# Row thresholds on VectorE, and four chunks transposed on TensorE: one change to a fused attention and feed-forward kernel

## The chip, the cores and the metric

One core of a Trainium2 chip. The metric is the device time of one execution in microseconds (us). Engines are named as in the profile: PE is TensorE, PEld its weight loads, DVE VectorE, ACT ScalarE, POOL GpSimd, SP SyncE, which here issues DMAs. All runs told of here were at a granted TensorE clock of 0.994 or more (0.998 or more in the profiled ones). Calls can land on different chips: the kernel before took 568.0, 570.0 and 567.5 us in three groups of runs, so kernels are compared by their ratio to the kernel before in the same rounds.

## The reference

```python
scores = q @ k.T / sqrt(64)                      # 8 batches x 8 heads, 576 x 576
thresh = max(scores, axis=-1) - tau              # tau = 0.02
scores = where(scores >= thresh, scores, -1e9)
x = softmax(scores) @ v                          # heads side by side: 4608 x 512
xn = x / sqrt(mean(x * x) + 1e-6) * rms_g
out = (silu(xn @ w_gate) * (xn @ w_val)) @ w_out # 512 -> 1536 -> 512
```

## The kernel before

The work is cut into 144 **steps** (128 query rows of two heads) and 36 **chunks** (128 rows of all eight heads, four steps). A step multiplies the scores into PSUM (`s_ps`, one buffer per head), VectorE copies them to SBUF as -score/8 and keeps each row's minimum in `mx`, and a tiny operation adds tau to it:

```python
nc.vector.tensor_tensor_reduce(                       # L589, once per head
    out=ssb[a][:, h], in0=s_ps[h][...], in1=zrow, scale=-1.0 / 8.0, scalar=3.0e38,
    op0=ALU.add, op1=ALU.min, accum_out=mx[m][:, h:h + 1])

def nthr(o):                                          # L596, the row threshold, 128x2
    nc.gpsimd.tensor_scalar(out=nth[m], in0=mx[m], scalar1=tau, scalar2=None, op0=ALU.add)
```

ScalarE then takes exponentials with `nth` as bias. From step 16 on, every second step leaves one head's mask to GpSimd: a comparison with `nth` ("mask", L640, 1.73 us) and a product with the exponentials ("take", L645, 1.28 us). After attention GpSimd norms a chunk's rows, and a transposing DMA (DMA_TRANSPOSE in the trace: in the median 1.2 us of the issuing queue and 2.5 us to landing) brings them to the feed-forward part (FFN):

```python
nc.sync.dma_start_transpose(out=xnT[slot][:, :, off:off + 128], in_=xn[ci % 2])   # L738, if ci >= N_XPE
...  # if ci < N_XPE: four TensorE transposes into PSUM, one VectorE copy to xnT
```

The order of instructions on each engine is not written by hand. The kernel lists all operations with a cost in nanoseconds (a table `COST`), plays them through a small list scheduler when it is built, and emits each engine's instructions in the order that comes out. So a changed entry in this table moves no work, but can move the order everywhere.

## Time and profile before

| | kernel before |
|---|---|
| time, median | 568.0 us (567.1 to 568.9, 5 runs) |
| TensorE, VectorE, ScalarE, GpSimd busy | 98%, 75%, 80%, 57% |
| threshold | 144 x 220 ns on GpSimd |
| transposes of normed rows | 36 by DMA |
| first FFN matmul | at 49.9 us |

A busy share is the time in which an engine shows an instruction, over the span. The threshold in the groups of instructions (busy us, mean ns, idle time before and what ended it):

```profile
L596 POOL TENSOR_SCALAR nth<-mx 128x2 f32<-128x2 f32 x144 | 31.6, 220 | 133.9 <-DVE mx L589 120.6
```

### The profile page before, as it was taken

What the parts mean: (1) busy time and instruction counts of PE and PEld (TensorE: products, weight loads), DVE (VectorE), ACT (ScalarE), POOL (GpSimd) and SP (SyncE); (2) the same over time, 40 slices, a digit from 0 to 9 for tenths busy, and PEclk for the clock granted to TensorE, in tenths of its full rate; (3) what the DMA queues carried; (4) which work ended last, traced back from release to release, by engine and by line L of the source; (5) the groups of instructions that cost most, each with busy time, mean ns of one, the idle gap of its engine ahead of it and who ended that gap; (6) DMA issues with size and microseconds to landing.
All of it is one profiled execution on the core that took longest, in us unless ns stands there. A gap on an engine that the chain in (4) does not pass through costs nothing.

```text
span 568.3 us, 13686 instructions
## 1 busy us (share of the span) xinstructions
PE 558.4 (98%) x5000; PEld 334.7 (59%) x5000; DVE 427.2 (75%) x1093; ACT 457.4 (80%) x739; POOL 322.4 (57%) x462
## 2 busy tenths in 40 slices
PE   8999999999999999999999999999999999999997
PEld 4666766767676555555555555545555455454674
DVE  4899977969958588758895789659875886586354
ACT  4999899999878787979898898778978897884332
POOL 2378946976747457666766658555666555551000
PEclk9999999999999999999999999999999999999999
DMA  8999998769994686999876799789887565633211
GB/s 187 250 289 282 178 195 184 161 132 202 167 202 104 136 159 149 177 177 187 178 160 148 142 186 181 161 168 162 174 167 184 88 96 86 178 81 44 84 37 38
DMA packets 270019, 88.98 MB, mean 157 GB/s; under 512 B 252544, under 2 KB 262272, under 8 KB 269952
## 3 DMA queue, kind: packets, MB, share of 16 engines
q1 hardware_dynamic: 267168, 86.02, 74.1%
q0 software_dynamic: 1600, 1.57, 1.8%
q8 instruction: 39, 0.64, 0.5%
q10 hardware_dynamic: 1184, 0.52, 0.3%
q14 instruction: 28, 0.23, 0.1%
HBM read 37.75 MB, written 9.44 MB: 83 GB/s over the span
## 4 chain that ended last, share of the span: by engine, by line
PE 89%; DVE 3%; DMA 2%; issue 2%; ACT 2%; POOL 1%; SPq 0%; DVEq 0%; POOLq 0%; ACTq 0%
PE s_ps L566 28%; PE ring L792 16%; PE ring L797 16%; PE ring L853 14%; PE ring L697 6%; PE ring L303 2%; PE ring L693 2%; DVE ssb L589 2%; DMA qkn<-in_q_dram 1%; PE s_ps L831 1%; PE s_ps L853 1%; PE ring L659 1%; PE s_ps L797 1%; PE ring L364 1%; DMA stage<-in_q_dram 1%
## 5 line engine op out<-in xcount | busy, mean ns | idle before, releaser
L589 DVE CUSTOM_DVE_ANT_0 ssb<-s_ps,zrow 128x576 f32<-128x576 f32 x288 | 207.8, 754 | 67.7 <-PE s_ps L566 60.5
L607 ACT ACTIVATE ssb<-ssb,nth 128x576 f32<-128x576 f32 x224 | 165.9, 766 | 32.4 <-POOL nth L596 32.1
L566 PE MATMUL s_ps<-qkt 64*128 64x288 f32 x1024 | 170.2, 429 | 1.4 <-DVE mx L589 1.1
L566 PEld LDWEIGHTS s_ps<-qkt 64*128 64x128 f32 x1024 | 96.2, 186 | 53.5 <-DVE mx L589 16.2
L640 POOL TENSOR_SCALAR wsb<-ssb,nth 128x576 f16<-128x576 f32 x64 | 110.5, 1726 | 9.7 <-DMA wt<-wsb 2.9
L792 PE MATMUL ring<-xnT,wg 128*128 128x512 f16 (+1 forms) x548 | 112.9, 328 | 0.4 <-DVE sl L809 0.4
L797 PE MATMUL ring<-xnT,wv 128*128 128x256 f16 (+1 forms) x544 | 111.4, 327 | 0.6 <-ACT qTv L472 0.3
L596 POOL TENSOR_SCALAR nth<-mx 128x2 f32<-128x2 f32 x144 | 31.6, 220 | 133.9 <-DVE mx L589 120.6
L809 DVE SCALAR_TENSOR_TENSOR sl<-th,ring 128x512 f32<-128x512 f32 (+1 forms) x137 | 75.9, 554 | 25.9 <-ACT th L806 24.6
L614 ACT ACTIVATE wsb<-ssb 128x1152 f16<-128x1152 f32 x80 | 92.9, 1161 | 1.9
L806 ACT ACTIVATE th<-ring 128x512 f32<-128x512 f32 (+1 forms) x137 | 66.3, 486 | 28.9 <-PE ring L792 26.4
L853 PE MATMUL ring<-wo,hf 128*128 128x512 f16 x384 | 89.3, 380 | 0.0
L645 POOL TENSOR_TENSOR wsb<-wsb,esb 128x576 f16<-128x576 f16 x64 | 81.8, 1278 | 8.8 <-ACT esb L626 4.4
L814 DVE TENSOR_TENSOR hf<-ring,sl 128x256 f16<-128x256 f32 (+1 forms) x136 | 75.9, 558 | 10.0 <-PE s_ps L566 0.5
L797 PEld LDWEIGHTS <-wv 128*128 128x128 f16 x576 | 52.2, 98 | 42.9 <-issue 12.3
L792 PEld LDWEIGHTS <-wg 128*128 128x128 f16 x576 | 52.0, 98 | 41.0 <-issue 11.6
L853 PEld LDWEIGHTS <-hf 128*128 128x128 f16 x408 | 37.4, 98 | 47.2 <-issue 6.6
L626 ACT ACTIVATE esb<-ssb,nth 128x576 f16<-128x576 f32 x64 | 49.2, 768 | 7.1 <-POOL nth L596 7.0
L697 PE MATMUL ring<-va,wt 128*128 128x65 f16 (+1 forms) x1264 | 52.8, 193 | 0.0
L697 PEld LDWEIGHTS <-wt 128*128 128x128 f16 (+1 forms) x1280 | 48.7, 100 | 3.4
L611 ACT ACTIVATE wsb<-ssb 128x576 f16<-128x576 f32 x64 | 43.6, 681 | 1.6
L693 PE MATMUL ring<-va,wt 128*128 128x130 f16 (+1 forms) x158 | 35.1, 227 | 0.1
(68 smaller groups left out, 448.1 us busy)
## 6 DMA issues: line engine op xcount, KB each, us to landing
vst<-in_v_dram SPq DMA_DIRECT2D x32, 256.0 KB, 3.2
qkn<-in_k_dram SPq DMA_DIRECT2D x31, 256.0 KB, 3.8
out_dram<-osb SPq DMA_DIRECT2D x31, 256.0 KB, 2.6
qkn<-in_q_dram SPq DMA_DIRECT2D x28, 256.0 KB, 4.1
stage<-in_moe_w_gate_dram SPq DMA_DIRECT2D x6, 512.0 KB, 6.6
stage<-in_moe_w_val_dram SPq DMA_DIRECT2D x6, 512.0 KB, 6.3
wt<-wsb SPq DMA_TRANSPOSE x128, 3.1
wo<-in_moe_w_out_dram POOLq DMA_DIRECT2D x4, 384.0 KB, 7.6
```

Of the source, the lines that this page charges most:

```text
L566: nc.tensor.matmul(s_ps[h][rows, ROW_AT + n * part:ROW_AT + n * part + n], lhs(hs), kT[i][p][h][hs, n * part:n * part + n], start=True, st ...
L589: nc.vector.tensor_tensor_reduce(out=ssb[a][:, h], in0=s_ps[h][:, ROW_AT:ROW_AT + S], in1=zrow, scale=-1.0 / 8.0, scalar=3.0e38, op0=ALU.a ...
L607: nc.scalar.activation(out=ssb[a][:, h], in_=ssb[a][:, h], func=PRELU, scale=-1.0, bias=nth[m][:, h:h + 1], **PRELU_KW)
L614: nc.scalar.activation(out=wsb[s % NW], in_=ssb[a], func=AF.Exp)
L640: nc.gpsimd.tensor_scalar(out=wsb[s % NW][:, h], in0=ssb[a][:, h], scalar1=nth[m][:, h:h + 1], scalar2=None, op0=ALU.is_le)
L645: nc.gpsimd.tensor_tensor(out=wsb[s % NW][:, h], in0=wsb[s % NW][:, h], in1=esb[es], op=ALU.mult)
L697: nc.tensor.matmul(ring[o.slot[0]][rs, at:at + D + 1], w[:, 5 * h + j, rs], va[vi][:, p, 2 * j + h], start=False, stop=(h == 1 and j == 3))
L792: nc.tensor.matmul(ring[o.slot[0]][:, 0:n], wg[d][:, fs], xnT[slot][:, d, 0:n], start=(d == 0), stop=(d == 3))
L797: nc.tensor.matmul(ring[o.slot[0]][:, 0:n], wv[d][:, fs], xnT[slot][:, d, 0:n], start=(d == 0), stop=(d == 3))
L809: nc.vector.scalar_tensor_tensor(out=sl[i][:, 0:n], in0=th[i][:, 0:n], scalar=1.0, in1=ring[g.slot[0]][:, 0:n], op0=ALU.add, op1=ALU.mult)
L814: nc.vector.tensor_tensor(out=hf[hi][:, 0:n], in0=ring[vv.slot[0]][:, 0:n], in1=sl[i][:, 0:n], op=ALU.mult)
L853: nc.tensor.matmul(ring[(first or o).slot[0]], hf[hs[fc][0]][:, 128 * j:128 * (j + 1)], wo[:, fc], start=(fc == 0), stop=(fc == NFC - 1))
```

## The change

It moves the threshold from the busy queue of GpSimd to VectorE, which has just made its input, so that ScalarE gets it sooner; it frees the early DMA queue of four DMA transposes so that the FFN can start earlier; and it brings three issue costs of the ordering table nearer to what was seen.

```diff
-    sp=480.0, sp_v=650.0, ..., sp_qk=900.0, ...
+    sp=420.0, sp_v=600.0, ..., sp_qk=680.0, ...
@@
-            nc.gpsimd.tensor_scalar(out=nth[m], in0=mx[m], scalar1=tau, scalar2=None, op0=ALU.add)
-        tn = add("POOL", COST["pool_tiny"], s - 4, ...)
+            (nc.gpsimd if NTH == "POOL" else nc.vector).tensor_scalar(
+                out=nth[m][:, lo:hi], in0=mx[m][:, lo:hi], scalar1=tau, scalar2=None, op0=ALU.add)
+        tns.append(add("POOL" if NTH == "POOL" else "DVE", ... else NTHC, s - 4, ...))
@@
+NTH = 'DVE'
+NTHC = 80.0
@@
-N_XPE = 0
+N_XPE = 4
```

(With `NTH = 'DVE'` there is one threshold operation per step, for both heads, as before.)

More of the change, by code (lines that the diff above doesn't have):

```diff
@@ L20 @@
     pool_tiny=270.0, pool_mean=800.0, pool_dma=850.0, cast_v=650.0, cast_vt=420.0, cast_w=720.0,
-    sp=480.0, sp_v=650.0, sp_w=600.0, sp_tr=1300.0, sp_qk=900.0, sp_tl=630.0,
+    sp=420.0, sp_v=600.0, sp_w=600.0, sp_tr=1300.0, sp_qk=680.0, sp_tl=630.0,
 )
@@ L593, in emit_softmax, with nthr @@
             ttr_of[s, h] = add("DVE", COST["ttr"], s - 1, [so, o_c] + exp_of.get(s - NSS, []), ttr)
-        def nthr(o):
-            nc.gpsimd.tensor_scalar(out=nth[m], in0=mx[m], scalar1=tau, scalar2=None, op0=ALU.add)
-        tn = add("POOL", COST["pool_tiny"], s - 4, [ttr_of[s, 0], ttr_of[s, 1]], nthr)
+        tns = []
+        for lo, hi in ((0, 1), (1, 2)) if NTH == "EACH" else ((0, 2),):
+            def nthr(o, lo=lo, hi=hi):
+                (nc.gpsimd if NTH == "POOL" else nc.vector).tensor_scalar(
+                    out=nth[m][:, lo:hi], in0=mx[m][:, lo:hi], scalar1=tau, scalar2=None, op0=ALU.add)
+            tns.append(add("POOL" if NTH == "POOL" else "DVE", COST["pool_tiny"] if NTH == "POOL" else NTHC, s - 4,
+                           [ttr_of[s, h] for h in range(lo, hi)], nthr))
         wfree = [w_read.get(s - NW)]
@@ L614, in ex2 @@
                     nc.scalar.activation(out=wsb[s % NW], in_=ssb[a], func=AF.Exp)
-                pls.append(add("ACT", COST["prelu"], s + 0.5, [tn], prelu))
+                pls.append(add("ACT", COST["prelu"], s + 0.5, [tns[h % len(tns)]], prelu))
                 if ways != "pp":
@@ L627, in ex @@
                                          bias=nth[m][:, h:h + 1])
-                e = add("ACT", COST["exp1"], s + 0.4, [tn, pre.get(("es", es))], ex)
+                e = add("ACT", COST["exp1"], s + 0.4, [tns[h % len(tns)], pre.get(("es", es))], ex)
                 if way == "d":
@@ L646, in take @@
                                                 op=ALU.mult)
-                    mk = add("POOL", COST["mask_g"], s + 0.4, [tn] + wfree, mask)
+                    mk = add("POOL", COST["mask_g"], s + 0.4, [tns[h % len(tns)]] + wfree, mask)
                     st = add("POOL", COST["take_g"], s + 0.4, [e, mk], take)
```

## The prediction

> **What bounds the kernel now.** I read the page from the top: busy shares, then the slices.
>
> ```profile
> PE 558.4 (98%) x5000; PEld 334.7 (59%) x5000; DVE 427.2 (75%) x1093; ACT 457.4 (80%) x739; POOL 322.4 (57%) x462
> ...
> PE   8999999999999999999999999999999999999997
> ...
> DVE  4899977969958588758895789659875886586354
> ACT  4999899999878787979898898778978897884332
> ...
> PEclk9999999999999999999999999999999999999999
> ```
>
> TensorE looks full from the second slice on, at full clock. [...] the groups by shape give 380 ns for one 512-column matmul, while in the chain of waits twelve of them in a row take 2.69 us, 224 ns each. So I asked differently: in the list of instructions in order of time I took, for each kind of TensorE block (eight score matmuls; four gate matmuls; and so on), the time from its start to the start of the next block, and its median: 1.17 us for a score block, 0.87 for four 512-column gate matmuls, 0.44 for four of 256 columns. What a block took above its median I call a stall (for the few kinds that come only a few times, above their shortest pace). The stalls sum to only 34.9 of 568 us: 7.9 before 20 us, 11.1 from 20 to 80, 2.9 from 160 to 180, 4.2 after the last matmul, and 8.8 in all the rest, about 0.5 us in each 20. So TensorE does work almost all of the time, and only stalls can be saved. The order in time shows both states of a score block (start, us, what):
>
> ```profile
> 47.53 1.91 PE L566 MATMUL s_ps<-qkt 64*128 64x288 f32 x8 [0.32 <-DVE mx L589]
> ...
> 304.67 1.24 PE L566 MATMUL s_ps<-qkt 64*128 64x288 f32 x8
> ```
>
> At 304.67 it runs through; at 47.53 its second half waits until VectorE has read the other head's old scores out of PSUM (s_ps is single). The busy times by stretch (PE, PEld, DVE, ACT, POOL, in us of 10 or 20) show why that happens early:
>
> ```profile
> 20.00:30.00 10.00, 9.03 (x127) 7.16 (x126) 9.05 (x26) 9.39 (x15) 3.90 (x8) 1.00 1.06 279
> 30.00:40.00 10.00, 8.94 (x116) 6.79 (x115) 8.95 (x25) 9.17 (x13) 7.99 (x17) 1.00 1.14 283
> 40.00:50.00 10.00, 9.57 (x95) 6.31 (x95) 9.16 (x28) 9.25 (x13) 8.67 (x17) 1.00 1.18 272
> 50.00:60.00 10.00, 10.00 (x111) 7.19 (x110) 9.54 (x29) 9.90 (x17) 7.99 (x15) 1.00 1.13 267
> ```
>
> Until about 60 us VectorE and ScalarE are at 90% and over, the DMA engines too (last two columns: DMA share, GB/s), and TensorE has no FFN work before 49.9 us.
>
> **The waits that the change aims at.** In the view of waits, us in total, times, longest:
>
> ```profile
> POOL nth L596 <- DVE mx L589: 120.6, 68, 9.3
> DVE ssb L589 <- PE s_ps L566: 60.5, 66, 2.6
> ACT ssb L607 <- POOL nth L596: 32.1, 39, 2.0
> ...
> ACT esb L626 <- POOL nth L596: 7.0, 13, 1.8
> ```
>
> ScalarE waits 39.1 us for the threshold, part of it because the 220 ns threshold stands in GpSimd's queue behind masks of 1.73 us and weight casts of 0.69 us. But ScalarE is 80% busy, and these waits hardly reach TensorE: the row above them shows VectorE itself waiting 60.5 us for scores. GpSimd's 120.6 us are idle time of an engine that sets nothing.
>
> **Part 1, 144 thresholds from GpSimd to VectorE.** Removed: 144 x 220 ns = 31.6 us of GpSimd, one hop between engines per step, and the queueing there. Added on VectorE: [...] the trace has 83 ns for the 128x1 accumulator read and 179 for the 128x4 reciprocal from PSUM. I take 80 ns: 144 x 0.08 = 11.5 us, and VectorE goes from 75% to 77%. From 80 us on, where TensorE stalls 0.5 us in 20, the shorter hop has nothing to shorten. Before 80 us ScalarE waits for thresholds 3.9 us between 20 and 80; some 20 steps lie there, so VectorE pays 20 x 0.08 = 1.6 us in the stretch where it is nearly full. I put the gain at 2 us and the cost at 1.5.
>
> **Part 2, four chunks transposed on TensorE.** Removed: 4 of 36 crossbar transposes (1.2 us of the issuing queue each, up to 2.5 early; 2.4 to 5.7 us to landing) out of the stretch with the fullest DMA, and the queue's halts in front of them: at 30, 42 and 55 us SyncE stands still for 1.6 to 3 us until the normed rows are there, with weight and q loads behind. Added: 16 matmuls. [...] this trace has nine transposes of the same shape in 0.51 us, 57 ns each at their pace (219 ns is the modelled length of one), and the measurement counts: 16 x 57 ns = 0.9 us, with about 0.09 us at each change of kind (a 512-column gate block takes 0.96 instead of 0.87 then) 1.3 us in all on the path that sets the end. VectorE gets four copies of 128x512 f16 at 416 ns, 1.7 us, where it is nearly full. In return the first FFN block can start before 49.9 us: its second chunk's normed rows are there at 43.8 us, the crossbar brings them about 2.5 us later; through TensorE and a copy they would be there after about 1 us. I expect the start 2 to 4 us earlier and 2 to 3 us of early stalls filled. q loads that land sooner could save part of one more stall (0.9 us at 35.9 us, where TensorE waits for a q load of 7.5 us).
>
> **Part 3, the static order.** Three costs of issuing are lowered in the table from which the kernel computes the order of all engines. No work changes; the order does, everywhere. With TensorE so full that moves little: I allow 2 us either way.
>
> Sum without a further wait: -2 + 1.5 + 1.3 - 2.5 - 0.5 = about -2 us, and at most some 10, since 11.1 us of early stalls are all there is to win apart from start and end.
>
> **Rivals.** (a) **A lock takes the wait's place.** [...] The kernel before shows nothing of it[...]. Estimate: GpSimd without thresholds is busy 291 us; its instructions, each with half its length as the mean rest (64 x 1.73 squared, 64 x 1.28 squared, the casts, norms and powers: 350 us squared in all), give 350 / 2 / 568 = 0.31 us of expected wait per threshold, 144 x 0.31 = 44 us, and VectorE would be occupied 85%. Most of it would fall into VectorE's waits for scores. From 250 to 300 us, though, VectorE is busy 43.1 of 50 us and would come near 94%; there silu and gate products come late, PSUM slots come free late and TensorE stalls. I let a fifth through: +9 us. (b) **VectorE becomes the early bound**: 3.2 us more work before 80 us lengthen that stretch by as much, and the earlier FFN start gives nothing, since its silu and gate products need VectorE too: +3 us. (c) **Hidden anyway**: the FFN is planned 16 steps behind its chunk, so a crossbar of 2.5 us is covered, and thresholds are off the path: 569 us. (d) **The early stalls go** for the most part: 558 us.
>
> **Range and chances.** Without the lock I get 566; with it about 575. A threshold beside GpSimd's masks would have been tried by whoever tuned this, and be kept only if it paid, so I give full effect of the lock a third or less, and (c) and (d) pull the other way: 567 us, 557 to 580. Over 2% means 11.4 us: as a gain it needs more than all early stalls, 5%; as a loss it needs the lock to reach TensorE with a quarter of its waits, 10%; within 2%, 85%.
>
> **What would show it.** In the changed profile: VectorE's threshold near 80 ns, no wait of ScalarE for GpSimd's threshold, GpSimd's busy time down by some 31 us; if (a) holds, a threshold of several hundred ns on average, long ones ending with GpSimd's mask. TensorE's first gate matmul before 48 us; 32 crossbar transposes of normed rows instead of 36; stalls of the score block between 20 and 60 us fewer if I am right, more under (b). From 80 us on TensorE's blocks at the same pace. I am wrong if TensorE stalls far more than 0.5 us in 20 there, or if the new order opens a gap such as the one at 166 to 176 us.

-2 + 1.5 + 1.3 - 2.5 - 0.5 is -2.2, "about -2 us", and so 566 from 568. The 80 ns behind the 1.5 are my estimate, near the 83 ns of the accumulator read in the trace. Rival (a) is a supposition, that a threshold on VectorE stands until the GpSimd instruction beside it ends, and an estimate of its waits from the lengths of GpSimd's instructions in the trace; the fifth of them that I let through is the +9 us that makes 575 of 566. "Lock" is my name for such a wait, "crossbar" for the transposing DMA.

## The result, and the profile after

The changed kernel took **573.4 us** (573.1 to 574.2, 5 runs) against 568.0 us: ratio 1.0096, 95% interval 1.0079 to 1.0113. A ratio here is the mean time of one kernel's fast runs over that of the other's fast runs of the same rounds, so it is not quite the ratio of the medians. Later the same kernel gave 1.0062 (run f1 below). It is a small loss, within 2%, and it is clear of noise.

The page of the changed kernel, its busy line and three of its costliest groups (busy us, mean ns, idle time before and what ended it):

```profile
PE 561.3 (98%) x5016; PEld 336.4 (59%) x5016; DVE 456.2 (80%) x1241; ACT 461.4 (81%) x739; POOL 290.0 (51%) x318
...
L611 ACT ACTIVATE ssb<-ssb,nth 128x576 f32<-128x576 f32 x224 | 165.7, 766 | 22.2 <-DVE nth L598 21.5
...
L630 ACT ACTIVATE esb<-ssb,nth 128x576 f16<-128x576 f32 x64 | 49.4, 772 | 15.5 <-DVE nth L598 14.9
...
L598 DVE TENSOR_SCALAR nth<-mx 128x2 f32<-128x2 f32 x144 | 34.8, 242 | 4.9
```

GpSimd lost 32.4 us of work, as it should. But VectorE gained 29.0, and the threshold takes 242 ns on average there, more than the 220 ns on GpSimd. ScalarE's wait for it hardly shrank: 21.5 + 14.9 = 36.4 us against 39.1.

The mean hides two kinds. The list of instructions in order of time (start, us, engine, line) shows a long threshold and a short one, 3.7 us apart:

```profile
115.21 1.28 POOL L649 TENSOR_TENSOR wsb<-wsb,esb 128x576 f16<-128x576 f16 x1
...
115.90 0.61 DVE L598 TENSOR_SCALAR nth<-mx 128x2 f32<-128x2 f32 x1
116.43 0.41 DVE L813 SCALAR_TENSOR_TENSOR sl<-th,ring 128x256 f32<-128x256 f32 x1
...
118.95 1.91 PE L566 MATMUL s_ps<-qkt 64*128 64x288 f32 x8
...
119.60 0.17 DVE L598 TENSOR_SCALAR nth<-mx 128x2 f32<-128x2 f32 x1
```

GpSimd's take runs from 115.21 to 116.49. The threshold begins at 115.90, while the take runs, and ends at 116.51, some 25 ns after it; the one at 119.60 finds GpSimd idle and needs 0.17 us. Behind the long one all of VectorE's queue is late, and the next score block to start, at 118.95, runs for 1.91 us: its second half waits. Of the 144 thresholds 111 took 157 to 195 ns, most of them 169 or 170; 33 took over 200 ns, up to 1.29 us, and nearly every one of them ended 22 to 28 ns after a GpSimd instruction: 24 after a take, 4 after a norm, 4 after a cast, 1 around a DMA issue. Taken over the median of 170 ns, the waits sum to 10.4 us. GpSimd's own masks and takes are as long as before (1.72 and 1.28 us on average), so it is VectorE that waits.

### The profile page after: what moved, and what is told of

Same layout as the page of the kernel before. It is cut to its first block, busy times and chain, and to the rows that moved or that the text cites. A ratio compares the mean times of both kernels' runs of the same rounds, so it can differ in the third digit from the quotient of the medians.

```text
span 571.1 us, 13669 instructions
## 1 busy us (share of the span) xinstructions
PE 561.3 (98%) x5016; PEld 336.4 (59%) x5016; DVE 456.2 (80%) x1241; ACT 461.4 (81%) x739; POOL 290.0 (51%) x318
## 4 chain that ended last, share of the span: by engine, by line
PE 88%; DVE 5%; DMA 4%; ACT 1%; issue 1%; SPq 0%; DVEq 0%
PE s_ps L566 27%; PE ring L796 16%; PE ring L801 15%; PE ring L857 15%; PE ring L701 6%; DMA qkn<-in_q_dram 4%; PE ring L303 2%; DVE ssb L589 2%; PE ring L697 2%; PE s_ps L801 1%; PE s_ps L835 1%; PE s_ps L857 1%; DMA stage<-in_q_dram 1%; DVE hf L818 1%; DVE nth L598 1%
## 5 line engine op out<-in xcount | busy, mean ns | idle before, releaser
L611 ACT ACTIVATE ssb<-ssb,nth 128x576 f32<-128x576 f32 x224 | 165.7, 766 | 22.2 <-DVE nth L598 21.5
L796 PE MATMUL ring<-xnT,wg 128*128 128x256 f16 (+1 forms) x564 | 114.5, 325 | 0.1
L801 PE MATMUL ring<-xnT,wv 128*128 128x512 f16 (+1 forms) x520 | 108.2, 330 | 0.2
L813 DVE SCALAR_TENSOR_TENSOR sl<-th,ring 128x256 f32<-128x256 f32 (+1 forms) x141 | 76.7, 544 | 19.9 <-ACT th L810 19.3
L810 ACT ACTIVATE th<-ring 128x256 f32<-128x256 f32 (+1 forms) x141 | 67.5, 480 | 28.4 <-PE ring L796 23.4
L818 DVE TENSOR_TENSOR hf<-ring,sl 128x512 f16<-128x512 f32 (+1 forms) x130 | 73.5, 566 | 10.5 <-PE ring L801 0.9
L630 ACT ACTIVATE esb<-ssb,nth 128x576 f16<-128x576 f32 x64 | 49.4, 772 | 15.5 <-DVE nth L598 14.9
L598 DVE TENSOR_SCALAR nth<-mx 128x2 f32<-128x2 f32 x144 | 34.8, 242 | 4.9
```

The lines of the kernel that those rows point to most:

```text
L611: nc.scalar.activation(out=ssb[a][:, h], in_=ssb[a][:, h], func=PRELU, scale=-1.0, bias=nth[m][:, h:h + 1], **PRELU_KW)
L796: nc.tensor.matmul(ring[o.slot[0]][:, 0:n], wg[d][:, fs], xnT[slot][:, d, 0:n], start=(d == 0), stop=(d == 3))
L801: nc.tensor.matmul(ring[o.slot[0]][:, 0:n], wv[d][:, fs], xnT[slot][:, d, 0:n], start=(d == 0), stop=(d == 3))
L813: nc.vector.scalar_tensor_tensor(out=sl[i][:, 0:n], in0=th[i][:, 0:n], scalar=1.0, in1=ring[g.slot[0]][:, 0:n], op0=ALU.add, op1=ALU.mult)
L818: nc.vector.tensor_tensor(out=hf[hi][:, 0:n], in0=ring[vv.slot[0]][:, 0:n], in1=sl[i][:, 0:n], op=ALU.mult)
```

## The experiments

All were correct. The first eight shared the runs of the kernel before (570.0 us), the last four had their own (567.5 us).

| run | thresholds | transposes on TensorE | issue costs | median us | ratio to before (95%) |
|---|---|---|---|---|---|
| e1 | GpSimd | 0 | new | 566.8 | 0.9951 (0.9934 to 0.9967) |
| e2 | VectorE | 0 | new | 571.9 | 1.0045 (1.0024 to 1.0066) |
| e3 | GpSimd | 4 | new | 568.0 | 0.9976 (0.9957 to 0.9994) |
| e4 | VectorE, as reduction | 4 | new | 569.2 | 0.9986 (0.9969 to 1.0004) |
| f1 | VectorE (the change) | 4 | new | 573.2 | 1.0062 (1.0044 to 1.0080) |
| f2 | reduction, twice | 4 | new | 570.7 | 1.0017 (1.0001 to 1.0032) |
| f3 | reduction, then tensor_scalar | 4 | new | 574.0 | 1.0075 (1.0059 to 1.0092) |
| f4 | VectorE | 4 | old | 577.3 | 1.0141 (1.0111 to 1.0172) |
| g1 | VectorE, cost entry 245 | 4 | new | 571.7 | 1.0067 (1.0049 to 1.0085) |
| g2 | GpSimd | 0 | half way | 568.1 | 1.0007 (0.9987 to 1.0027) |
| g3 | GpSimd | 0 | old, other order | 568.3 | 1.0007 (0.9989 to 1.0025) |
| g4 | GpSimd | 0 | new, other order | 566.6 | 0.9975 (0.9957 to 0.9992) |

My theory after the result was LOCK: the threshold stands until a running take, norm or cast of GpSimd ends, as in the trace above, and this reaches TensorE. What in the hardware makes it stand, no run shows. Its rivals were OWN TIME (any added VectorE time counts), TRANSPOSES, and ORDER (the new table entries gave a worse order).

**One part at a time (e1, e2, e3).**

```diff
 e1: NTH = 'POOL', N_XPE = 0     # only the three issue costs are new
 e2: NTH = 'DVE',  N_XPE = 0
 e3: NTH = 'POOL', N_XPE = 4
```

> Only the three issue costs in the ordering table are new; thresholds on GpSimd, no transposes on TensorE. ORDER theory (the new static order alone loses the 5.3 us): 572 to 574 us. LOCK, OWN TIME and TRANSPOSE theories (the work itself costs it): 567 to 569 us, as before.

> The change without the four transposes on TensorE (all 36 chunks through the crossbar). If the thresholds cost the time (LOCK or OWN TIME): 572 to 573.5 us, threshold mean near 240 ns on VectorE. If the TRANSPOSES cost it: 568 to 569 us. ORDER: about as e1.

> The change with the thresholds back on GpSimd, the four transposes on TensorE. If the TRANSPOSES cost the time: 571 to 574 us. If the thresholds cost it: 567 to 569.5 us (1.1 us of added TensorE work, perhaps won back). ORDER: about as e1.

e1 is not slower but 0.5% faster, so ORDER falls for the three issue costs. From e1 to e3 the transposes cost 1.2 us by the medians, from e1 to e2 the thresholds cost 5.1. Added up, -3.2 + 5.1 + 1.2 = +3.1 us, and the change showed +3.2 on this chip. So the loss is the thresholds, and part of it is hidden by a gain from the costs.

**The same threshold as a reduction (e4).** `mx` gets a second column per head that holds tau, and the threshold is a reduction over the pair. Order and everything else stay: in the traces of f1 and e4 the instructions of VectorE, ScalarE and GpSimd come in the same order, but for six memsets of tau at the start, and TensorE's differ in four records.

```diff
-mx = [sb(f"mx{i}", [128, 2]) ...]
+mx = [sb(f"mx{i}", [128, 2, 2]) ...]              # [:, :, 1] is set to tau once
-    nc.vector.tensor_scalar(out=nth[m], in0=mx[m], scalar1=tau, op0=ALU.add)
+    nc.vector.tensor_reduce(out=nth[m], in_=mx[m], axis=X, op=ALU.add)
```

> The whole change in the same static order, but the threshold is a VectorE reduction over pairs (row extreme, tau)[...]. If LOCK holds: no threshold over 200 ns, none ending with a GpSimd instruction, and the time 569 to 571.5 us. If the waits for the lock are absorbed by VectorE's idle time: thresholds short, yet the time within 0.8 us of the change's 573.4. If there is no such lock: the long thresholds stay.

The view of the tile `nth` of e4, and of the thresholds of the changed kernel (duration in ns: minimum, median, maximum; first and last start):

```profile
L600 DVE TENSOR_REDUCE nth<-mx x144: 145/157/159, 10.0 to 508.2; 128x2 f32<-128x4 f32 x144
```

```profile
L598 DVE TENSOR_SCALAR nth<-mx x144: 157/170/1292, 10.0 to 511.6; 128x2 f32<-128x2 f32 x144
```

No reduction took more than 159 ns. The time fell from 573.2 (f1) to 569.2 us: 4.0 of the 5.1 us that the thresholds cost are gone, in the same order of instructions, so ORDER falls here too. The same step as above, in order of time in e4:

```profile
114.23 0.08 DVE L591 DVE_READ_ACCUMULATOR2_ANT mx<- 128x1 f32 x1
114.23 0.75 DVE L591 CUSTOM_DVE_ANT_0 ssb<-s_ps,zrow 128x576 f32<-128x576 f32 x1
...
114.34 1.28 POOL L650 TENSOR_TENSOR wsb<-wsb,esb 128x576 f16<-128x576 f16 x1
114.91 0.08 DVE L591 DVE_READ_ACCUMULATOR2_ANT mx<- 128x1 f32 x1
115.03 0.16 DVE L600 TENSOR_REDUCE nth<-mx 128x2 f32<-128x4 f32 x1
115.10 0.41 DVE L814 SCALAR_TENSOR_TENSOR sl<-th,ring 128x256 f32<-128x256 f32 x1
...
118.16 1.38 PE L568 MATMUL s_ps<-qkt 64*128 64x288 f32 x8
```

The take runs from 114.34 to 115.62 again, right across the threshold, which takes no notice of it. The next gate product starts at 115.10 instead of 0.5 us later, and the score block at 118.16 runs 1.38 us instead of 1.91.

These lines also show what a short threshold costs VectorE's queue, which is not its recorded length. Without one in between, the next instruction starts together with the accumulator read (114.23); with one, it starts 0.11 us after the read's end (115.10 against 114.99), as the threshold needs what is read. Over the whole traces the next instruction starts 192 ns later in the median for a reduction and 195 for a tensor_scalar that does not wait: nearly the same, so in its own time e4 hardly differs from the change, while the waits are gone.

**Own time or waits (f1, f2, f3).** By the recorded lengths e4 also has 12 us less VectorE time than the change, so I took OWN TIME to be still open. f2 and f3 add 144 operations of nearly equal length (147 and 158 ns in the median) to e4, writing to a tile that nobody reads: f2 reductions, of which none waited in e4 (159 ns at most), f3 tensor_scalars, of which 33 of 144 took over 200 ns in the change. f1 is the change itself on this chip.

```diff
     nc.vector.tensor_reduce(out=nth[m], in_=mx[m], axis=X, op=ALU.add)
+f2: nc.vector.tensor_reduce(out=nth2[m], in_=mx[m], axis=X, op=ALU.add)
+f3: nc.vector.tensor_scalar(out=nth2[m], in0=mx[m][:, :, 0], scalar1=tau, op0=ALU.add)
```

> The changed kernel itself, on the same chip as the three below: 1.010 of before. Everything below is compared with it and with e4's reduction form.

> e4 with every reduction issued twice (the second into an unused tile): 144 x 157 ns = 22.6 us more work on VectorE[...]. OWN TIME theory (VectorE's added microseconds count wherever they come from; e4 to the change is 12 us of VectorE time and 1.1% of time): at least 1.2% over e4. LOCK theory (only the long, bunched waits count): within 0.5% of e4.

> e4 with a tensor_scalar into an unused tile behind every reduction: the threshold itself is early and lock-free[...]. LOCK through VectorE's queue: 0.6 to 1.2% over f2, which has the same count of instructions. LOCK through the late threshold (ScalarE and GpSimd get it late): within 0.3% of f2.

The busy lines of e4, f2 and f3, then the groups by shape of f2 and of f3:

```profile
PE 558.0 (98%) x5016; PEld 334.3 (59%) x5016; DVE 446.2 (79%) x1247; ACT 461.4 (81%) x739; POOL 290.7 (51%) x318
PE 560.7 (99%) x5016; PEld 336.6 (59%) x5016; DVE 453.7 (80%) x1391; ACT 461.0 (81%) x739; POOL 289.9 (51%) x318
PE 562.3 (98%) x5016; PEld 337.2 (59%) x5016; DVE 463.1 (81%) x1391; ACT 461.5 (81%) x739; POOL 290.1 (51%) x318
```

```profile
L601 DVE TENSOR_REDUCE nth<-mx 128x2 f32<-128x4 f32 x144 | 22.6, 157 | 4.9
L602 DVE TENSOR_REDUCE nth<-mx 128x2 f32<-128x4 f32 x144 | 21.1, 147 | 0.0
```

```profile
L602 DVE TENSOR_SCALAR nth<-mx 128x2 f32<-128x2 f32 x144 | 31.7, 220 | 0.0
L601 DVE TENSOR_REDUCE nth<-mx 128x2 f32<-128x4 f32 x144 | 22.6, 157 | 4.9
```

The second reductions are recorded with 21.1 us, but overlap their neighbours: VectorE's busy time rises by 453.7 - 446.2 = 7.5 us, and the time by 1.5 us (f2 against e4). The tensor_scalar is recorded with 31.7 - 21.1 = 10.6 us more than that second reduction, 8.9 of it over its median of 158 ns; the busy time rises by another 9.4 us, and the time by another 3.3 (f3 against f2). So a microsecond of plain work cost about 1.5 / 7.5 = 0.20 us, and a microsecond of waiting about 3.3 / 8.9 = 0.37. With the noise of a few tenths in either difference, that is about twice as much, not more. OWN TIME falls as the main cause, above all by e4 against e3: reductions that hold the queue as long as the change's thresholds, waits left out, cost 1.2 us where the change costs 5.2. And since in f3 the threshold itself is early (its reductions took 159 ns at most, the tensor_scalars behind them up to 1266) and only VectorE's queue stands, it is the queue behind the wait that costs, not the late threshold; that part of the theory was a guess before this run.

**Is it a bad order? (f4, g1).** f4 puts the old issue costs back under the change; g1 tells the ordering table what a threshold really takes.

```diff
 f4:  sp=480.0, sp_v=650.0, sp_qk=900.0
 g1:  NTHC = 245.0
```

> The change with the three issue costs of the ordering table put back. If the order that the new costs give is worth 0.5% here too, as e1 showed alone: 1.013 to 1.017 of before. If e1's gain is chance of one order: anywhere within 1% of the change.

> The change with the threshold's entry in the ordering table raised from 80 to 245 ns, what it took on average. If a wrong table entry made the order bad: 0.995 to 1.000 of before. If the lock and the work themselves cost it, whatever the order plans: 1.003 to 1.012 of before.

With the true cost in the table the ratio is 1.0067, with 80 ns it was 1.0062 and 1.0096: an order that allows for the mean does not cure it. The wait comes at some steps and not at others, and a mean is not what any one of them takes. The old costs are 0.8% worse under the change (0.7% by the medians; one of f4's runs took 582.2 us), 0.5% worse without it.

**What an order is worth by chance (g2, g3, g4).** The costs' gain was the part that I understood least. g3 moves an entry that the change never touches, which alone reorders TensorE's list nearly as much as the three new costs do (compared line by line, the matmuls in the traces differ from the kernel before's in 1,572 lines, against 1,928 in e1).

```diff
 g2 (from before): sp=450.0, sp_v=625.0, sp_qk=790.0
 g3 (from before): sq=805.0      # was 800
 g4 (from e1):     ttr=694.0     # was 690
```

> The kernel before with its three issue costs moved half way to the new ones. If the new costs help because they are truer: 0.996 to 0.9985 of before. If e1's 0.5% is chance: anywhere from 0.992 to 1.008.

> The kernel before with one entry of the ordering table that the change doesn't touch moved by 5 ns (of 800): no work changes, the order of all engines does, about as much as by the change's three costs. It measures what chance orders are worth: within 0.2% of before if orders matter little, up to 0.8% either way if e1's gain is chance.

> e1 with one entry that the change doesn't touch moved by 4 ns (of 690). If the new costs themselves are worth 0.5%: 0.993 to 0.998 of before, like e1. If e1's order was a lucky one: near 1.000.

The other old order is worth 0.07%, within noise, half way as well; the other new order is 0.25% faster than before where e1 was 0.49%. Two of two orders with the full new costs beat the kernel before, so they probably are worth something; how much of the 0.5% is e1's luck is not settled, as two orders on two chips are too few. Either way e1 and g4, which leave the thresholds and the transposes alone, are the fastest kernels here: 566.8 and 566.6 us, faster than both the kernel before and the change.

**Where TensorE lost it.** I took each kind of block at its clear pace (score block 1.17 us, 512-column matmul 0.216, and so on), called the sum work and the rest stalls, in us of the profiled spans:

| | work | stalls | 20-80 us | 80-180 | 180-300 | 300-500 |
|---|---|---|---|---|---|---|
| before | 524.3 | 44.0 | 11.6 | 7.2 | 5.1 | 6.5 |
| e1, costs only | 524.3 | 41.3 | 10.6 | 7.5 | 3.3 | 7.1 |
| e3, + transposes | 525.2 | 40.5 | 10.6 | 7.1 | 3.4 | 7.1 |
| e4, + reductions on VectorE | 525.2 | 42.6 | 12.5 | 6.8 | 3.8 | 6.7 |
| the change | 525.2 | 45.9 | 13.2 | 8.7 | 4.5 | 6.7 |
| f3 | 525.2 | 47.8 | 14.0 | 8.7 | 4.5 | 7.7 |

(This measure is stricter than the prediction's, which took medians and so counted 34.9 for the kernel before; the profiled run of before was at 570.2 us a slow one of its fast runs, so its stalls are some 1 to 2 us high. e1's profiled run was 0.6 us above its median and e3's 0.4 below, so their stalls can't be compared to better than 1 us.) From e4 to the change 2.6 of the 3.3 us come between 80 and 300 us, where 6.1 of the 10.4 us of waits lie; after 300 us waits of 2.7 us cost nothing. The busy times by stretch of the change show the two stages (PE, PEld, DVE, ACT, POOL):

```profile
60.00:180.00 120.00, 119.51 (x1220) 82.75 (x1218) 103.73 (x302) 104.87 (x180) 69.90 (x71) 1.00 0.79 160
180.00:300.00 120.00, 120.00 (x1061) 67.31 (x1058) 100.45 (x263) 102.22 (x160) 67.18 (x71) 1.00 0.82 159
300.00:500.00 200.00, 200.00 (x1749) 107.70 (x1748) 158.67 (x425) 172.30 (x266) 113.43 (x114) 1.00 0.77 153
```

VectorE is busy 86%, then 84%, then 79%. I read this so: a wait costs where VectorE has little time to catch up before TensorE needs a PSUM buffer back. No run tests this reading by itself.

**The earlier FFN start.** It came. Instructions of the gate matmul, duration and first and last start, before, then in the change:

```profile
L792 PE MATMUL ring<-xnT,wg x548: 269/378/390, 49.9 to 561.0; 128*128 128x512 f16 x95, 128*128 128x256 f16 x88
```

```profile
L796 PE MATMUL ring<-xnT,wg x564: 269/283/390, 45.9 to 563.5; 128*128 128x256 f16 x96, 128*128 128x512 f16 x92
```

In e3, which has the transposes alone, the first one is at 45.5 us too. Yet between e1 and e3 the stalls from 20 to 80 us are 10.6 and 10.6: four microseconds earlier filled nothing that this measure shows, and the added work was paid (0.9 us at the clear pace, 1.0 with the changes of kind).

## Why the prediction was right or wrong

The time, 573.4, lies in the range of 557 to 580, and "within 2%" was the forecast at 85%. But the middle was 6 us too low and on the wrong side of the kernel before, and the sum behind it has wrong terms that partly cancel; that the time still fell well inside a range of 23 us is in part luck.

- **What bounds the kernel: right.** After 80 us TensorE stalls little in every run, and no run moved by more than 1.5%.
- **"I put the gain at 2 us and the cost at 1.5" for the thresholds: the gain did not come.** Without the lock (e4 against e3) they cost 1.2 us, and the stalls from 20 to 80 us rose from 10.6 to 12.5. That fits rival (b), an early stretch bound by VectorE, in part; no run tests it by itself.
- **"I take 80 ns" for a threshold: wrong.** Alone it is recorded with 170 ns (157 at least), and it held VectorE's queue for 195, since it starts only after the accumulator read (35 ns after its end in the median). The 80 ns were my estimate, with the 83 ns of the accumulator read as support, an instruction for which the trace names no tile that it reads (`mx<-`). The error itself was cheap: all of e4's reductions, which hold the queue as long, cost 1.2 us.
- **"The kernel before shows nothing of it", rival (a): the lock was real, and it decided the sign.** The kernel before shows nothing of it indeed: none of its groups of VectorE instructions of one line and shape spreads by more than 14 ns. I gave the lock's full effect "a third or less" on the ground that whoever tuned this would have kept a threshold there "only if it paid". That was a guess about people, with no measurement behind it. In the trace of the change 24 of 33 long thresholds ended just after GpSimd's take.
- **"0.31 us of expected wait per threshold", 44 us in all: four times too much.** Measured 10.4. I let thresholds meet GpSimd's instructions at random moments. They don't: no long threshold met a mask, since each mask waits for the threshold just before it and, with its take, is done 3.2 us later, about when the next threshold comes (in e2's order two of 36 did meet one). So also "long ones ending with GpSimd's mask" was wrong: they end with the take.
- **"I let a fifth through": too little.** About 0.37 of the waits reached TensorE. The two errors partly cancel, to 3.3 to 4.0 us in place of 9, and without the lock the time fell by 0.8 us (e4, within noise) in place of 2; that 575 with the lock was not far off is luck, not insight.
- **"2 to 3 us of early stalls filled" by the transposes: wrong.** The first gate matmul came 4 us earlier, as foreseen, and nothing was filled; rival (b) had said why, as silu and gate products need VectorE too, and this stands as the likely reason, not as a shown one. The cost, 1.3 us estimated, was 1.1 in the profile and 1.2 in the time.
- **"I allow 2 us either way" for the order: a little small.** It was -2.8 us on one chip, and a part of it may be chance.
- **"No wait of ScalarE for GpSimd's threshold": true and empty.** It waited 36.4 us for VectorE's instead.

## What to carry to other kernels

Before a small operation is moved to VectorE, ask whether it waits there for another engine: here a tensor_scalar of 128x2 from SBUF to SBUF stood behind GpSimd's takes, norms and casts (33 of 144 took over 200 ns), and the same sum written as a reduction did not (159 ns at most), for 4 us of 573. Waiting in VectorE's queue was passed on to the time more than plain work was: here 0.37 us of each microsecond against 0.20. And read what an instruction costs a queue from the start of the next one, or from what it adds to the busy time, not from its recorded length: a threshold recorded with 170 ns held the queue for 195 behind an accumulator read, and f2's second reductions, recorded with 147 ns each, added 52 each to VectorE's busy time (7.5 us over 144). And where a scheduler computes the order, measure what a chance order is worth, and make each comparison in the same order, before a small gain is put down to a part of the change.
